# Local and global attention with a routed MLP: four transposes of the gate moved ahead of the output matmuls

## Chip, cores and metric

The kernel runs on one core of a Trainium2 chip. The metric is the device time of one execution in microseconds (us); the lower the better.

## What is computed

For 8 batches and 8 heads of width 64, 512 local tokens attend to a window of 32 tokens either side and to 32 global tokens; the 32 global tokens attend to everything. The 4352 resulting rows of 512 numbers then go through a gate (512 to 8), a greedy assignment of every row to one of 8 experts by sorted gate values, and the expert's two-layer MLP.

```
a_l = sm(where(|i-j| <= 32, scale * q_l @ k_l.T, -1e9) ++ scale * q_l @ k_g.T)
out_l = a_l @ concat(v_g, v_l)
out_g = sm(scale * q_g @ concat(k_g, k_l).T) @ concat(v_g, v_l)
x = concat(out_g, out_l) as rows of 512
logits = x @ w_gate ; greedy assignment, 544 rows for each of 8 experts
out[rows of e] = relu(x @ w1[e]) @ w2[e]
```

## The kernel before, in words

The program is written out in order for each engine, and each engine runs its own list in order. Attention comes first and takes the first 200 us of the trace; routing and the experts follow and are not touched.

Attention is a pipeline of 40 steps. Each batch has five: four local ones (a pair of heads each) and a global one. In iteration `i` three steps are worked on at once: the scores of step `i + 2` (`S`), the transposes of the probabilities of step `i` (`T0`, `T1`, one for each head, four 128x128 turns each), the masks and exponentials of step `i + 2` (`M0`, `M1`), and the output matmuls and normalisations of step `i - 1` (`O0`, `O1`). The order within an iteration is a string, `STEADY = "S T0 T1 M0 M1 O0 O1 G"`. TensorE (PE) does S, T, O; VectorE (DVE) the masks (L175), for a global step the maxima (L236 to L238), and the normalisations (L202 to L207, L278 to L282); ScalarE (ACT) the exponentials (L180, L244, L246) and the evacuation of the turns of p to `pt` and `pgt` (L314).

`G`, at the end of an iteration, does the pieces of the gate that are listed in `extra` for it. For each batch `b`, with `s0 = 5 * (b + 1)`:

- `gate_x` for c = 0 to 3, in iterations s0 to s0 + 3: four transposes of a column block of `xs` (the normalised outputs of a whole batch) into a PSUM tile `T`, and its evacuation to `xt` by DVE (L316, 682 ns);
- `turn_xg` in s0 + 1: one transpose of the global outputs `xg`, and its evacuation by DVE;
- `gate_m` in s0 + 4 (matmuls with the gate's weights, evacuated by ACT to `ltc`), and `gate_l` in s0 + 5 (four transposes of `ltc`, and a reduction on DVE to `L`). Iteration s0 + 5 is also the first of the next batch's `gate_x`;
- `gate_g` and its `gate_l` for the global rows once in four batches.

Batch 6 is compressed (two column blocks in each of iterations 35 and 36), and batch 7 has places of its own.

PSUM is full: three banks of `S`, three of `T`, two of `O`. A new `T` tile gets the bank that was released longest ago in program order; its first writer waits for the last reader of the tile that had the bank. Both heads of a step take a `T` tile each, a global step four, and `glob_scores` takes one too: the small scores `sb` of the second global head lie in a `T` tile from S on, until the last exponential of `M1` (L246) has read them. That is in iteration s0 + 2.

Loads and stores go out on SyncE's queue. Every PE instruction adds to a count of work (`tick`); each 0.62 us of it issues one piece of a load or store (`piece`), made to wait for the PE instruction before it (`paced`).

Of the kernel before, what the change touches and what calls it, by code (L numbers as in the profile page):

```python
# [13 lines left out]
ALU = mybir.AluOpType  # L14
AX = mybir.AxisListType
# [4 lines left out]
S = SL + SG  # L20
# [25 lines left out]
@with_exitstack  # L46
def block(ctx, tc, A, out, nbatch=B, dump=None):
    nc = tc.nc
    ctx.enter_context(tc.manual_schedule())
    consts = ctx.enter_context(tc.tile_pool(name="consts", bufs=1))  # L50
    dram = ctx.enter_context(tc.tile_pool(name="dram", bufs=1, space=DRAM))
    xd = dram.tile([N, DM], F32, name="xd")

    ident = consts.tile([128, 128], F32, name="ident")
    L = consts.tile([128, 34, E], F32, name="L")
    if dump is not None:
        nc.vector.memset(L, 0.0)
    rt = Routing(tc, A, consts, L, ident) if out is not None else None
    if rt:
        rt.begin(ctx)  # L60
    attention(tc, A, consts, xd, ident, L, nbatch, rt)
    if dump is not None:
        nc.sync.dma_start(dump["L"], L.rearrange("p a b -> p (a b)"))
        nc.sync.dma_start(dump["x"][:nbatch * S], xd[:nbatch * S])
    if out is not None:
        rt.begin_ps(ctx)
        experts(tc, A, xd, ident, rt, out)
# [3 lines left out]
def attention(ctx, tc, A, consts, xd, ident, L, nbatch, rt=None):  # L71
    nc = tc.nc
# [238 lines left out]
    def evac(dst, src, k):  # L311
        nev[k] += 1
        if who[k][nev[k] % len(who[k])] == "A" and not (k == "p" and nev[k] <= 2):
            nc.scalar.activation(dst, src, AF.Copy)  # L314
        else:
            nc.vector.tensor_copy(dst, src)  # L316

    def gate_x(src, xt, c, spare):
        t = ps.tile([128, NB, 128], F32, name="S" if spare else "T", bufs=3 if spare else 3)
        n = src.shape[1]  # L320
        for k in range(n):
            pe.transpose(t[:, k, :], src[:, k, c * 128:(c + 1) * 128], ident)
        evac(xt[:, c, :n * 128], t[:, :n].rearrange("p a b -> p (a b)"), "l" if late[0] else "x")

    def gate_m(xt, n):
        lt = ps.tile([128, 512], F32, name="T", bufs=3)
        for c in range(4):
            pe.matmul(lt[32 * c:32 * c + 32, :n * 128], wg[:, c, :], xt[:, c, :n * 128],
                             start=True, stop=True)
        ltc = wk.tile([128, 512], F32, name="ltc", bufs=2)  # L330
        evac(ltc[:, :n * 128], lt[:, :n * 128], "l")
        return ltc

    def gate_l(ltc, J, n):
        t = ps.tile([128, NB, 4, 32], F32, name="T", bufs=3)
        for k in range(n):
            pe.transpose(t[:, k].rearrange("p a b -> p (a b)"), ltc[:, k * 128:(k + 1) * 128], ident)
        nc.vector.tensor_reduce(L[:, J:J + n, :], t[:, :n, :, 0:8].rearrange("p k c e -> p k e c"),
                                axis=AX.X, op=ALU.add)

    def gate_d(xt, c):
        if c == 0:
            lt.append(ps.tile([128, NB, E], F32, name="T", bufs=3))
        for k in range(NB):
            pe.matmul(lt[0][:, k], xt[:, c, 128 * k:128 * k + 128], wg[:, c, 0:E], start=(c + k == 0), stop=(c + k == 6))
        if c == 3:
            nc.scalar.activation(L[:, 4 * nbatch - 4:4 * nbatch], lt[0], AF.Copy)
# [3 lines left out]
    def gate_units(b, src, J, n):  # L351
        xt = []

        def go(c):
            if c == 0:
                xt.append(wk.tile([128, 4, 128 * n], F32, name=f"xt{n}", bufs=1))
            if c < 4:
                gate_x(src(), xt[0], c, b == nbatch - 1)
            elif b == nbatch - 1:
                gate_d(xt[0], c - 4)  # L360
            elif c == 4:
                xt.append(gate_m(xt[0], n))
            else:
                gate_l(xt[1], J, n)
        return [lambda c=c: go(c) for c in range(8 if b == nbatch - 1 else 6)]

    late = [False]
    gxt = {}

    def turn_xg(b):  # L370
        if b % 4 == 0:
            gxt[b // 4] = wk.tile([128, 4, 128], F32, name="xt1", bufs=1)
        t = ps.tile([128, NB, 128], F32, name="S" if b == nbatch - 1 else "T", bufs=3)
        pe.transpose(t[:, 0, :], xg[b].rearrange("p a b -> p (a b)"), ident)
        q = 32 * (b % 4)
        evac(gxt[b // 4][:, :, q:q + 32], t[:, 0].rearrange("p (a b) -> p a b", a=4), "l" if late[0] else "x")

    def gate_g(i):
        gxt[i] = gate_m(gxt[i], 1)
# [8 lines left out]
    extra = {}  # L388

    def put(i, slot, f):  # L390
        extra.setdefault((i, slot), []).append(f)
    for b in range(nbatch):
        last = b == nbatch - 1
        s0 = 5 * (b + 1)
        put(s0 - 2 if last else s0 + 1, 0, lambda b=b: turn_xg(b))
        if b % 4 == 3:
            put(s0 - 1 if last else s0 + 3, 0, lambda b=b: gate_g(b // 4))
            put(s0 if last else s0 + 4, 0, lambda b=b: gate_l(gxt[b // 4], 32 + b // 4, 1))
        lo = gate_units(b, lambda b=b: xs[b], 4 * b, NB)
        if last:  # L400
            put(s0 - 3, 0, lo[0])
            put(s0 - 1, 0, lo[1])
            put(s0, 0, lo[2])
            for f in [lo[4], lo[3]] + lo[5:]:
                put(s0, 2, f)
        else:
            fast = b == nbatch - 2
            for k in range(4):
                put(s0 + (k // 2 if fast else k), 0, lo[k])
            put(s0 + (2 if fast else 4), 0, lo[4])  # L410
            put(s0 + (3 if fast else 5), 0, lo[5])

    LA = 2
    RAMP = 2
    START, STEADY = "T0 T1 O0 O1 S M0 M1 G", "S T0 T1 M0 M1 O0 O1 G"

    need, left = {}, {}
    for i, u in enumerate(steps):
        for q in [u[0].q] if isinstance(u[0], Local) else range(NP):
            for f, t in ((load_qk, i - LA), (load_v, i + 1)):  # L420
                k = f, u[0].b, q
# [8 lines left out]
    def used(f, u):  # L430
        for q in [u[0].q] if isinstance(u[0], Local) else range(NP):
            left[f, u[0].b, q] -= 1
            live[f] -= left[f, u[0].b, q] == 0

    now_ = [-LA]
# [32 lines left out]
    for i in range(-LA, ns + 1):  # L468
        if rt and i == 4:
            rt.load()  # L470
        if rt and i == 9:
            rt.prepare()
        nx = steps[i + LA] if i + LA < ns else []
        cur = steps[i] if 0 <= i < ns else []
        old = steps[i - 1] if i > 0 else []
        if i < RAMP:
            order = START
        else:
            order = STEADY
        late[0] = i >= ns - 1  # L480
        for n, what in enumerate(order.split()):
            now_[0] = i + n / 8
            if what == "S" and nx:
                (local_scores if isinstance(nx[0], Local) else glob_scores)(nx)
                used(load_qk, nx)
            if what[0] == "T" and cur:
                cur[int(what[1])].turn()
                cur[int(what[1])].take()
            if what[0] == "M" and nx:
                nx[int(what[1])].mask()  # L490
                nx[int(what[1])].exp()
            if what[0] == "O" and old:
                old[int(what[1])].out()
                if what[1] == "1":
                    used(load_v, old)
                old[int(what[1])].norm()
            if what == "G":
                if rt and i == ns:
                    for _ in first:
                        pass  # L500
                    rt.digits(slice(0, 28))
                for slot in range(3):
                    for f in extra.get((i, slot), []):
                        f()


WARM = 10
# [804 lines left out]
```

## Time and profile before

| | |
|---|---|
| median of 3 runs | 690.2 us (689.28 to 691.4) |
| the profiled execution | 689.55 us |
| its span, first to last instruction | 687.8 us |
| PE busy over the span | 642.6 us (93%) |
| DVE, ACT, GpSimd busy | 460.7 us (67%), 307.4 us (45%), 246.4 us (36%) |
| mean granted TensorE clock | 0.976 of full |

The engines are averaged over attention, routing and experts together; what a change in attention is worth has to be read from the first 200 us.

### The profile page before, as it was taken

The page shows a single profiled execution, that of the slowest core. Times are in us where ns is not written, and L with a number is a line of the kernel's source. Part 1 is how long each engine was busy: PE and PEld are TensorE (multiplying, and loading weights), DVE is VectorE, ACT ScalarE, POOL GpSimd, SP SyncE. Part 2 cuts the span into 40 slices and gives each one's busy share as a digit, 9 for nine tenths or more (in the row PEclk, how much of TensorE's full clock was granted, in tenths as well). Part 3 has the DMA queues.
Part 4 walks back from the last instruction along what each step waited for, and adds up shares of the span by engine and source line. Part 5 has one row for each costly group of instructions (what it writes and reads, how often), then busy time and mean ns, then how long its engine had stood idle before and what let it go on. Part 6 is the DMA issues. An engine that isn't in the chain of part 4 may idle for free.

```text
span 687.8 us, 24694 instructions
## 1 busy us (share of the span) xinstructions
PE 642.6 (93%) x10356; PEld 538.6 (78%) x10356; DVE 460.7 (67%) x1765; ACT 307.4 (45%) x828; POOL 246.4 (36%) x314
## 2 busy tenths in 40 slices
PE   7888999999982899999999999999999999999996
PEld 6676777767761798789789879878978978988985
DVE  4788788778876898777668758767857762640410
ACT  4776867777730352443333334334423343542410
POOL 4786667686600412411511330141141143312011
PEclk9999999999995799999999999999999999999999
DMA  7677878776210442603331440361352236431001
GB/s 242 206 244 226 227 228 242 242 218 200 89 68 2 137 175 91 255 32 124 110 144 39 143 177 22 128 202 48 124 163 91 80 114 238 134 127 54 9 15 51
DMA packets 41119, 93.91 MB, mean 137 GB/s; under 512 B 5424, under 2 KB 28208, under 8 KB 36912
## 3 DMA queue, kind: packets, MB, share of 16 engines
q0 software_dynamic: 10240, 51.39, 21.6%
q1 hardware_dynamic: 30768, 40.95, 19.5%
q8 instruction: 81, 1.33, 0.8%
q14 instruction: 30, 0.25, 0.1%
HBM read 74.49 MB, written 17.83 MB: 134 GB/s over the span
## 4 chain that ended last, share of the span: by engine, by line
PE 89%; DVE 4%; DMA 3%; issue 3%; ACT 1%; SPq 0%; POOLq 0%; POOL 0%; ACTq 0%
PE H L1135 29%; PE Y L1090 27%; PE T L90 11%; PE S L90 7%; PE O L90 7%; PE R L632 4%; PE H L967 2%; PE Y L1098 2%; DMA xg<-xd,idx 1%; DMA qk<-in_qk_dram 1%; DVE r_pm L554 1%; DMA mask<-in_mask_dram 1%; DVE r_G L554 0%; DMA out_dram<-y,idx 0%; DVE r_ce L554 0%
## 5 line engine op out<-in xcount | busy, mean ns | idle before, releaser
L1135 PE MATMUL H<-xh,w1h 128*128 128x272 f32 (+2 forms) x512 | 149.8, 294 | 0.9 <-DVE hl L554 0.6
L1135 PE MATMUL H<-xh,w1l 128*128 128x272 f32 (+2 forms) x512 | 149.9, 294 | 0.0
L1135 PE MATMUL H<-xl,w1h 128*128 128x272 f32 (+2 forms) x512 | 148.4, 291 | 0.0
L979 POOL DMA_INDIRECT out_dram<-y,idx x40 | 40.8, 1019 | 179.4 <-ACT y L1078 102.8
L1137 ACT ACTIVATE hh<-H 128x272 fp32r<-128x272 f32 (+2 forms) x128 | 50.8, 397 | 119.4 <-PE H L1135 115.9
L1090 PE MATMUL Y<-w2h,hh 128*128 128x512 f32 x256 | 103.7, 405 | 0.0
L1090 PE MATMUL Y<-w2l,hh 128*128 128x512 f32 x256 | 103.5, 404 | 0.0
L1090 PE MATMUL Y<-w2h,hl 128*128 128x512 f32 x256 | 103.4, 404 | 0.0
L1135 PEld LDWEIGHTS H<-xh,w1h 128*128 128x128 f32 x512 | 96.3, 189 | 2.3 <-DVE hl L554 1.4
L1135 PEld LDWEIGHTS H<-xl,w1h 128*128 128x128 f32 x512 | 96.3, 188 | 0.5
L1135 PEld LDWEIGHTS H<-xh,w1l 128*128 128x128 f32 x512 | 96.1, 188 | 0.5
L126 POOL COPY vw<-vw 32x650 f32<-32x650 f32 x96 | 69.3, 722 | 52.4 <-DMA vw<-in_vw_dram 33.7
L180 ACT ACTIVATE p<-p,nm 128x128 f32<-128x128 f32 x256 | 78.0, 397 | 8.5 <-DVE nm L175 8.5
L1078 ACT ACTIVATE y<-Y 128x512 f32<-128x512 f32 (+1 forms) x40 | 21.3, 533 | 122.9 <-PE Y L1090 79.5
L554 DVE SCALAR_TENSOR_TENSOR hl<-H,hh 128x272 fp32r<-128x272 f32 (+2 forms) x128 | 55.1, 434 | 30.6 <-ACT h L1139 18.6
L175 DVE CUSTOM_DVE_ANT_0 p<-S,mask 128x128 f32<-128x128 f32 x256 | 56.5, 286 | 24.2 <-PE S L90 22.8
L90 PE MATMUL S<-qk 64*32 64x128 f32 (+2 forms) x2240 | 52.6, 293 | 9.3 <-issue 5.1
L554 DVE TENSOR_TENSOR w2l<-w2r,w2h 128x512 fp32r<-128x512 f32 x64 | 42.8, 682 | 25.3 <-ACT w2h L933 25.3
L920 POOL DMA_INDIRECT xg<-xd,idx x40 | 42.9, 1073 | 37.4 <-DVE idx L554 23.2
L1090 PEld LDWEIGHTS Y<-w2h,hh 128*128 128x128 f32 x256 | 48.1, 188 | 10.4 <-issue 1.2
L1090 PEld LDWEIGHTS Y<-w2h,hl 128*128 128x128 f32 x256 | 48.2, 188 | 9.3
L1090 PEld LDWEIGHTS Y<-w2l,hh 128*128 128x128 f32 x256 | 48.2, 188 | 9.0
(180 smaller groups left out, 1116.4 us busy)
## 6 DMA issues: line engine op xcount, KB each, us to landing
qk<-in_qk_dram SPq DMA_DIRECT2D x64, 204.0 KB, 3.0
vw<-in_vw_dram SPq DMA_DIRECT2D x64, 162.5 KB, 3.3
xd<-xs SPq DMA_DIRECT2D x28, 256.0 KB, 3.4
qk<-in_qk_dram SPq DMA_DIRECT2D x32, 200.0 KB, 3.2
xd<-xs SPq DMA_DIRECT2D x1, 1024.0 KB
xg<-xd,idx POOLq DMA_INDIRECT x40
out_dram<-y,idx POOLq DMA_INDIRECT x40
vw<-in_ve_dram SPq DMA_DIRECT2D x32, 16.2 KB, 3.8
```

The costliest lines, as they stand in the source:

```text
L90: s.last = op(o, w, x, **kw)
L126: copy(bv[32 * g:32 * g + 32], av[32 * g + 32:32 * g + 64])
L175: nc.vector.tensor_tensor_reduce(s.p[:, c, :], s.st[:, c, :], mask[:, c, :], -SCALE, BIG, ALU.add, ALU.min, s.nm[:, c:c + 1])
L180: nc.scalar.activation(s.p[:, c, :], s.p[:, c, :], AF.Exp, bias=s.nm[:, c:c + 1], scale=-1.0)
L554: return op(*args, **kw)
L632: s.nc.tensor.matmul(out, *args, **kw)
L920: nc.gpsimd.indirect_dma_start(out=dst, out_offset=None, in_=src, element_offset=off, in_offset=bass.IndirectOffsetOnAxis(ap=idx, axis=0))
L979: nc.gpsimd.indirect_dma_start(out=out4 if t == 4 else out, out_offset=bass.IndirectOffsetOnAxis(ap=rt.idx[ph][:, k:k + 1], axis=0), in_=y ...
L1078: nc.scalar.activation(y, p[:, :w], AF.Copy)
L1090: nc.tensor.matmul(p, h[:, f, q], w[f], start=(f + k == 0), stop=(f + k == 9))
L1135: nc.tensor.matmul(p, w[d][:, fs], x[:, d, q], start=(n == 0), stop=(n == 11))
L1137: nc.scalar.activation(hh[:, f, q], p, AF.Relu)
```

## The change

The four transposes of `gate_x` get a place of their own in the order, `X`, straight behind `T1`; their evacuation gets another, `Y`, behind `O1`. This holds for c = 0 to 3 of batches 0 to 5 and c = 0 and 2 of batch 6, 26 in all. Everything else of the gate stays in `G`, and so do the transposes of batch 7 and c = 1 and 3 of batch 6. `gate_x` and `gate_l` now return their evacuation, which `G` calls at once. The fraction of an iteration that the load planner uses as its clock is in tenths now, in the steady order, and not in eighths.

```diff
@@ gate_x
-        evac(xt[:, c, :n * 128], t[:, :n].rearrange("p a b -> p (a b)"), "l" if late[0] else "x")
+        k = "l" if late[0] else "x"
+        return lambda: evac(xt[:, c, :n * 128], t[:, :n].rearrange("p a b -> p (a b)"), k)
@@ gate_l
-        nc.vector.tensor_reduce(L[:, J:J + n, :], t[:, :n, :, 0:8].rearrange("p k c e -> p k e c"),
-                                axis=AX.X, op=ALU.add)
+        return lambda: nc.vector.tensor_reduce(L[:, J:J + n, :], t[:, :n, :, 0:8].rearrange("p k c e -> p k e c"),
+                                               axis=AX.X, op=ALU.add)
@@ gate_units, go
-                gate_x(src(), xt[0], c, b == nbatch - 1)
+                return gate_x(src(), xt[0], c, b == nbatch - 1)
...
-                gate_l(xt[1], J, n)
+                return gate_l(xt[1], J, n)
@@ attention
-                put(s0 + (k // 2 if fast else k), 0, lo[k])
+                put(s0 + (k // 2 if fast else k), 0 if fast and k % 2 else "X", lo[k])
...
-    START, STEADY = "T0 T1 O0 O1 S M0 M1 G", "S T0 T1 M0 M1 O0 O1 G"
+    START, STEADY = "T0 T1 O0 O1 S M0 M1 G", "S T0 T1 X M0 M1 O0 O1 Y G"
...
-            now_[0] = i + n / 8
+            now_[0] = i + n / len(order.split())
+            if what == "X":
+                turned = [f() for f in extra.get((i, "X"), [])]
+            if what == "Y":
+                for f in turned:
+                    f()
...
-                        f()
+                        f = f()
+                        if f:
+                            f()
```

## Rows read from the trace of the kernel before

**Rows 1.** The page: the chain that ended last, share of the span by line.

```profile
PE H L1135 29%; PE Y L1090 27%; PE T L90 11%; PE S L90 7%; PE O L90 7%; PE R L632 4%; PE H L967 2%; PE Y L1098 2%; DMA xg<-xd,idx 1%; DMA qk<-in_qk_dram 1%; DVE r_pm L554 1%; DMA mask<-in_mask_dram 1%; DVE r_G L554 0%; DMA out_dram<-y,idx 0%; DVE r_ce L554 0%
```

**Rows 2.** Four steps of attention: busy us (instructions) of each engine, clock, DMA.

```profile
88.50:105.62 17.12, 16.76 (x539) 12.61 (x537) 14.60 (x82) 13.82 (x43) 10.64 (x17) 1.00 0.70 216
```

**Rows 3.** Waits of PE and its weight loads, 20 to 200 us: us, times, longest.

```profile
PE S L90 <- issue: 5.1, 7, 1.3
...
PEld S L90 <- DMA qk<-in_qk_dram: 1.7, 2, 0.8
...
PEld T L90 <- DVE xt L316: 0.2, 1, 0.2
```

**Rows 4.** Weight loads in order of time, iterations 16 to 19: start, us, [idle before].

```profile
88.50 0.86 PEld L90 LDWEIGHTS T<-ident,p 128*128 128x128 f32 x8 [0.20 <-issue]
...
91.26 0.27 PEld L90 LDWEIGHTS S<-qk 64*32 64x32 f32 x24 [0.17 <-issue]
...
92.39 0.85 PEld L90 LDWEIGHTS T<-ident,p 128*128 128x128 f32 x8
93.41 0.95 PEld L90 LDWEIGHTS O<-vw,pt 128*32 128x32 f32 x64 [0.17 <-issue]
94.46 0.42 PEld L90 LDWEIGHTS T<-ident,xs 128*128 128x128 f32 x4
95.04 0.82 PEld L90 LDWEIGHTS S<-qk 64*32 64x32 f32 x51 [0.17 <-ACT pg L244]
96.10 0.18 PEld L90 LDWEIGHTS S<-qk 64*32 64x32 f32 x13 [0.24 <-issue]
96.48 0.85 PEld L90 LDWEIGHTS T<-ident,p 128*128 128x128 f32 x8 [0.20 <-issue]
...
100.89 1.08 PEld L90 LDWEIGHTS T<-ident,pg 128*128 128x128 f32 x10 [0.20 <-ACT p L180]
102.24 0.20 PEld L90 LDWEIGHTS T<-ident,pg 128*128 128x128 f32 x2 [0.27 <-ACT pgt L314]
102.61 0.95 PEld L90 LDWEIGHTS O<-vw,pt 128*32 128x32 f32 x64 [0.17 <-issue]
...
104.51 0.91 PEld L90 LDWEIGHTS S<-qk 64*32 64x32 f32 x64 [0.84 <-issue]
105.62 0.85 PEld L90 LDWEIGHTS T<-ident,p 128*128 128x128 f32 x8 [0.20 <-ACT p L180]
```

**Rows 5.** The same in an early iteration that has nothing in G.

```profile
26.27 0.95 PEld L90 LDWEIGHTS O<-vw,pt 128*32 128x32 f32 x64 [0.17 <-issue]
27.32 0.14 PEld L90 LDWEIGHTS S<-qk 64*32 64x32 f32 x3
```

**Rows 6.** DVE in order of time, iterations 16 to 19.

```profile
88.60 0.29 DVE L175 CUSTOM_DVE_ANT_0 p<-S,mask 128x128 f32<-128x128 f32 x1 [1.85 <-PE S L90]
...
90.30 0.16 DVE L202 TENSOR_SCALAR ls<-O 128x4 f32<-128x4 f32 x1
...
91.78 0.88 DVE L316 COPY xt<-T 128x128 f32<-128x128 f32 x2
92.58 0.65 DVE L236 TENSOR_REDUCE gm<-S 128x1 f32<-128x480 f32 x1
...
94.46 0.15 DVE L202 TENSOR_SCALAR ls<-O 128x4 f32<-128x4 f32 x1
...
95.94 0.68 DVE L316 COPY xt<-T 128x512 f32<-128x512 f32 x1
96.72 0.29 DVE L175 CUSTOM_DVE_ANT_0 p<-S,mask 128x128 f32<-128x128 f32 x1
...
103.34 0.16 DVE L202 TENSOR_SCALAR ls<-O 128x4 f32<-128x4 f32 x1 [0.43 <-PE O L90]
```

**Rows 7.** ACT in order of time, iteration 17.

```profile
93.08 1.09 ACT L314 ACTIVATE pt<-T 128x512 f32<-128x512 f32 x2 [0.42 <-PE T L90]
...
95.63 0.33 ACT L246 ACTIVATE pg<-T,gm 128x64 f32<-128x64 f32 x1
```

## The prediction

> **What bounds the kernel now.** I read the chain that ended last first: within attention it is PE alone that appears with weight, T 11%, S 7% and O 7% of the span [rows 1]. Then four iterations in the middle of attention, 88.50 to 105.62: PE is busy 16.76 of 17.12 us, DVE 14.60, ACT 13.82 [rows 2]. So PE sets the pace, and DVE follows closely. What PE waits for is hardly ever another engine: scores wait 5.1 us in all for nothing that the profile shows ("issue"), 1.7 us for a load, and turns 0.2 us for an evacuation by DVE [rows 3]. The weight loads in order of time give the pitch of every part of an iteration [rows 4], and DVE's and ACT's lists beside them show how late the readers of the T tiles run [rows 6, 7].
>
> **What the change takes away.** 26 groups of four turns move; each instruction stays. Eight turns and the step to the outputs last 93.41 - 92.39 = 1.02 us, with 0.17 idle before the outputs: (1.02 - 0.17) / 8 = 0.107 for a turn [rows 4]. Four turns of xs behind the outputs last 95.04 - 94.46 = 0.58, which is 4 x 0.107 = 0.43 and 0.15 for the step from whole-array turns back to tiled scores. The outputs last 1.05 before turns (94.46 - 93.41) and 1.05 before scores (27.32 - 26.27) [rows 4, 5], so once the turns follow those of p, that 0.15 is gone: T T X O S has one step fewer than T T O X S. It goes only where G holds no other PE work. In s0 + 1 the turn of xg stays there, in s0 (from batch 1 on) the turns of ltc, in iteration 23 gate_g, and in 35 and 36 several. Left are iteration 5, six at s0 + 2 and five at s0 + 3: 12 x 0.15 = 1.8 us.
>
> The rows show these steps as idle weight loads of 0.17 to 0.20 [rows 4]. [...]
>
> **What it adds: the outputs come 0.43 us later.** They are behind the moved turns now, so O0's result comes at 1.45 + 0.73 = 2.18 us after the first turn of p (1.02 + 0.43; 0.73 is 103.34 - 102.61, outputs to DVE's first read) [rows 4, 6]. DVE's list is unchanged: masks 1.70 (88.60 to 90.30) or global maxima 1.88 (92.58 to 94.46), two normalisations 1.48 (94.46 to 95.94), the evacuation 0.78 to the next instruction (95.94 to 96.72) and 0.68 by itself [rows 6]. In iteration 16 the masks end at 1.80 after T0; DVE will stand idle to 2.18. That delay of 0.38 goes into the evacuation of xt, and two things now wait for readers of T tiles. Take iterations 16 to 19, and T0 of 16 as zero.
>
> Iteration 16 (s0 + 1). Normalisations 2.18 to 3.66, evacuation of xs to 4.34, of xg behind it. PE: outputs from 1.45 to 2.50, the turn of xg and the step to S 0.107 + 0.17, global scores 92.39 - 91.26 = 1.13 [rows 4]: T0 of 17 could start at 3.91 (before: 3.89). But sb takes the bank of T1, xg that of T0, so T0 of 17 gets the bank of the moved turns, whose reader ends at 4.34. With 0.05 allowed for the signal (my estimate; without it every wait below is 0.05 shorter) it starts at 4.39, 0.50 later than before. Before, T0's bank was xg's, read earlier than xs.
>
> Iteration 17 (s0 + 2). One bank holds sb until L246 has read it, 95.63 + 0.33 - 92.39 = 3.57 after T0 [rows 4, 7]. The moved turns come when only T0's bank is free, and its evacuation starts 0.69 after T0 (93.08 - 92.39) [rows 4, 7]. The row nearest to this wait is that of the global step, where a turn waits for the evacuation of a tile filled just before: the turn starts 102.24 - 100.89 = 1.35 after the first [rows 4]. The moved turns would follow at 0.86, so PE stands 0.48. Queued behind them: both outputs, so both normalisations. Before, the same turns, on the same bank, came at 94.46, behind the outputs, and waited for nothing. Iteration: 1.34 + 0.43 + 0.17 + 1.05 + 1.11 = 4.10 (S 1.11: 105.62 - 104.51) [rows 4]. Before it lasted 4.09 with an idle 0.24 in S; if that stays too, the price is 0.25.
>
> Iteration 18 (s0 + 3). 1.45 + 1.05 + 1.11 = 3.61, against 1.02 + 1.05 + 0.58 + 1.11 = 3.76. DVE runs late meanwhile: in 17 its normalisations begin at 1.94 + 0.73 = 2.67, the next masks at 2.67 + 1.48 + 0.78 = 4.93, which is 0.83 into 18; they end at 2.53, and the evacuation at 2.53 + 1.48 + 0.68 = 4.69, 1.08 into 19.
>
> Iteration 19 (global, s0 + 4). Its third T tile has the bank of 18's moved turns: 1.13 instead of 6 x 0.107 = 0.64. Of this 0.49, the 0.27 that the fourth tile waited anyway is covered; 0.22 remains. Then DVE has no xt to evacuate, and its delay is gone.
>
> Sum for the batch: 0.50 + 0.25 - 0.15 + 0.22 = 0.82 us slower. **Bounds.** Below: iterations 16 to 20 took 17.12 us [rows 2], with 0.24 and, in iteration 18, 4.41 - 3.76 = 0.65 of idle time that no engine caused. If such gaps fall while DVE catches up, waits of up to that size cost nothing, and only the saved steps remain, 0.30 a batch at s0 + 2 and s0 + 3: from -0.30. Above: 0.82 with all gaps besides. I take 0.60, nearer the upper end, since half of the gaps or more would fall elsewhere. Six batches (0 to 5) have the pattern: 6 x 0.60 = 3.6, less 0.15 for iteration 5. **+3.5 us.**
>
> **What moves at no cost.** The moved turns issue no DMA themselves, but their ticks do: a piece of a load may go out half an iteration earlier, and the planner's clock runs in tenths. SyncE's queue stays in order, each piece still behind a PE instruction. The loads' slack covers it: scores waited twice for qk, 1.7 us in all [rows 3]; without that cover a late load cost 0.8. The reduction of gate_l and all ACT work keep their places. PE's clock was granted in full throughout these steps [rows 2], and gaps of half a microsecond do not lengthen the longest that it had (1.3) [rows 3].
>
> Against the profiled execution of 689.55 us the sum gives 693.05. That execution is 0.65 below the median of the three; I put the forecast between, at **693.3 us**.
>
> **Rivals.**
> 1. *The issue gaps take the waits' place.* For it: 5.1 us of them before scores alone [rows 3], and 0.89 in the four iterations above, about the size of 0.82. Against it: they would have to fall behind the outputs of s0 + 1 or within s0 + 2. Time: the four iterations go from 17.12 to 17.12 - 0.89 + 0.82 = 17.05 plus the gaps that stay outside, so from -1.8 us to +2 in all, about 690.
> 2. *Fewer steps between tilings decide; faster.* If the turn of xg or ltc left in G costs PE less than a whole step, all 26 groups save 0.15: 3.9 us, 686.3; with the 12 alone 688.4. It decides from the point where the two waits of s0 + 1 and s0 + 2 fall under (3.9 - 2.1) / 6 = 0.3 us a batch together, of the 0.98 reckoned above. For it: turns waited for xt once, 0.2 us [rows 3]. Against: DVE's starts follow each other without a gap from 88.60 to 96.72 [rows 6], and the 0.48 for ACT does not hang on DVE.
> 3. *The moved turns of s0 + 2 get sb's bank.* They would start at 3.57 + 0.05 instead of 0.86 (8 x 0.107), 2.76 us for PE, six times: 16.6 us, 707. Against: before, the turns at 94.46 ran while L246 still had to read sb at 95.63 [rows 4, 7], so they had another bank.
>
> [...]
>
> **How the numbers follow.** Chances: the waits bind (forecast, 691.5 to 695.5) 0.47; rival 1 0.33; rival 2 0.16; rival 3 0.04. Faster or slower by over 0.3% (2.07 us, about what this kernel's measurement can tell from no change) means under 688.1 or over 692.3: faster 0.16, same 0.33, slower 0.51. The range leaves out rival 3, most of rival 2 and a little above: 688.0 to 695.8; the likeliest case's own is 691.5 to 695.5.
>
> **What would show it.** Right: in s0 + 1 to s0 + 2 the weight loads of T0 wait some 0.5 us for DVE's xt; in s0 + 2 the turns of xs wait about 0.5 for ACT's pt; at s0 + 3 outputs go to scores in 1.05 with nothing between; DVE waits for O about 0.4 in s0 + 1. Wrong: the wait for xt stays at some tenths of a microsecond in all; or attention ends earlier though the waits are there, which would mean that the gaps shrank. A different bank for the turns, or loads that come late by the planner's new clock, would make the sum wrong outright.

## The result and the profile after

The change takes 695.29 us (median of 17 runs) where the kernel before takes 691.4 beside it (17 runs): ratio 1.0067, 95% interval 1.005 to 1.0084, slower. At 690 us that is 4.6 us, with 3.5 to 5.8 by the interval; the two medians alone, from which the ratio is not formed, lie 3.9 apart. The forecast was 3.5 against the profiled execution, at the lower end of the interval. Of the 2.0 us between the forecast of 693.3 and 695.29, 1.2 lie in the kernel before, whose median was 690.2 when the forecast was made. The profiled execution of the change is a long one among its runs (699.22 us, span 697.4), so single times of its trace are compared by their places, and sizes by several profiles.

The weight loads in order of time, iterations 16 to 19 of the change; they answer to [rows 4].

```profile
94.86 0.86 PEld L90 LDWEIGHTS T<-ident,p 128*128 128x128 f32 x8 [0.20 <-issue]
95.69 0.47 PEld L90 LDWEIGHTS T<-ident,xs 128*128 128x128 f32 x4
96.33 0.95 PEld L90 LDWEIGHTS O<-vw,pt 128*32 128x32 f32 x64 [0.17 <-issue]
...
99.34 0.85 PEld L90 LDWEIGHTS T<-ident,p 128*128 128x128 f32 x8 [0.70 <-PE T L90]
100.69 0.42 PEld L90 LDWEIGHTS T<-ident,xs 128*128 128x128 f32 x4 [0.49 <-ACT pt L314]
101.27 0.95 PEld L90 LDWEIGHTS O<-vw,pt 128*32 128x32 f32 x64 [0.17 <-issue]
102.32 0.89 PEld L90 LDWEIGHTS S<-qk 64*32 64x32 f32 x64
103.40 0.85 PEld L90 LDWEIGHTS T<-ident,p 128*128 128x128 f32 x8 [0.20 <-issue]
...
105.92 0.57 PEld L90 LDWEIGHTS S<-qk 64*32 64x32 f32 x35
107.94 0.39 PEld L90 LDWEIGHTS S<-qk 64*32 64x32 f32 x29 [1.45 <-issue]
108.54 1.07 PEld L90 LDWEIGHTS T<-ident,pg 128*128 128x128 f32 x10 [0.20 <-issue]
109.88 0.20 PEld L90 LDWEIGHTS T<-ident,pg 128*128 128x128 f32 x2 [0.27 <-ACT pgt L314]
...
113.26 0.86 PEld L90 LDWEIGHTS T<-ident,p 128*128 128x128 f32 x8 [0.20 <-ACT p L180]
```

Both waits stand where the prediction put them. T0 of s0 + 2 (99.34) waits 0.70, where no idle time stood before (92.39 in [rows 4]); then the turns of xs wait 0.49 for `pt`. The idle time of 0.70 carries the name "PE T", but those turns had long ended; VectorE's list shows what did end then:

```profile
97.06 0.16 DVE L202 TENSOR_SCALAR ls<-O 128x4 f32<-128x4 f32 x1 [0.31 <-PE O L90]
...
98.55 0.88 DVE L316 COPY xt<-T 128x512 f32<-128x512 f32 x2
...
102.00 0.16 DVE L202 TENSOR_SCALAR ls<-O 128x4 f32<-128x4 f32 x1 [0.69 <-PE O L90]
```

The copy of xs begins at 98.55 and takes 0.68 by itself [rows 6], to 99.23; T0 starts at 99.34. VectorE, which had no idle time at these places before, stands for the outputs 0.31 and 0.69.

The four iterations, from one first turn to the next, in us. "Less gaps" leaves out issue idle time before scores and outputs beyond the usual 0.2 (before 0.24 and 0.65, after 1.51: scores took 108.54 - 105.92 = 2.62 instead of 1.11).

| | before, less gaps | forecast, undiscounted | after, less gaps |
|---|---|---|---|
| s0 + 1 | 3.89 | 4.39 | 4.48 |
| s0 + 2 | 3.85 | 4.10 | 4.06 |
| s0 + 3 | 3.76 | 3.61 | 3.63 |
| s0 + 4 | 4.73 | 4.95 | 4.72 |
| sum | 16.23 | 17.05 | 16.89 |

With the gaps the same stretch took 17.12 us before [rows 2], and now:

```profile
94.86:113.26 18.40, 16.37 (x539) 12.50 (x537) 14.70 (x82) 13.82 (x43) 11.63 (x18) 1.00 0.66 200
```

The same instructions on PE and VectorE, the clock granted in full, and 1.28 us more. Nearly all of the difference between the two profiled executions lies ahead of routing, whose first matmul starts at 210.9 us (before 202.3): 8.6 of the 9.6 us between the spans. From there to the end they take 486.5 and 485.5 us. These two executions lie further apart than the kernels do.

### The profile page after: what moved, and what is told of

It reads as the page before. It is cut to its first block, busy times and chain, and to the rows that moved or that the text cites. A ratio compares the mean times of both kernels' runs of the same rounds, so it can differ in the third digit from the quotient of the medians.

```text
span 697.4 us, 24703 instructions
## 1 busy us (share of the span) xinstructions
PE 644.3 (92%) x10356; PEld 540.1 (77%) x10356; DVE 461.4 (66%) x1765; ACT 308.2 (44%) x828; POOL 246.9 (35%) x314
## 4 chain that ended last, share of the span: by engine, by line
PE 85%; DVE 6%; issue 3%; DMA 2%; POOL 1%; ACT 1%; SPq 1%; POOLq 0%; ACTq 0%; DVEq 0%
PE H L1143 28%; PE Y L1098 27%; PE T L90 9%; PE O L90 6%; PE S L90 5%; PE R L640 4%; PE H L975 2%; PE Y L1106 2%; DMA vw<-in_vw_dram 1%; PE Y L1176 1%; DVE r_pm L562 1%; POOL vw L126 1%; DVE xs L207 1%; DVE r_G L562 1%; ACT pt L314 1%
## 5 line engine op out<-in xcount | busy, mean ns | idle before, releaser
L1098 PEld LDWEIGHTS Y<-w2h,hh 128*128 128x128 f32 x256 | 48.2, 188 | 10.6 <-issue 1.2
```

The costliest lines, as they stand in the source:

```text
L1098: nc.tensor.matmul(p, h[:, f, q], w[f], start=(f + k == 0), stop=(f + k == 9))
```

## The experiments

Three theories went into the expectations. Theory 1: the two waits for the readers of `T` tiles make the difference. Theory 2: the loads, which the planner's new clock issues at other times, make it. Theory 3: TensorE's issue gaps make it. These turned out to recur at every 256th instruction of its list (a weight load and its matmul are two); the rows are in the last section.

### Each wait taken away, and both

`evac_early`: the evacuation ahead of O0, so that VectorE reads the tile before it waits for outputs.

```diff
-    START, STEADY = "T0 T1 O0 O1 S M0 M1 G", "S T0 T1 X M0 M1 O0 O1 Y G"
+    START, STEADY = "T0 T1 O0 O1 S M0 M1 G", "S T0 T1 X M0 M1 Y O0 O1 G"
```

> The evacuation of the moved turns stands in front of the outputs' normalisations on VectorE (Y ahead of O0) instead of behind them; PE and ACT keep the order of the changed kernel. Theory 1, waits for T tiles: VectorE fills the 0.4 us in which it stood idle for the outputs, the bank is free 1.2 us earlier, so the turns of p in iteration s0 + 2 wait for nothing (0.5 us a batch back) and the third tile of the global step neither (0.2); the wait of the turns of xs for pt stays (0.49). Six times 0.7 us off 695.3: about 691 us, ratio to before 0.999 to 1.003. Theory 2, the loads: the pieces go out at other places and PE's issue gaps grow; VectorE's order does not touch that, ratio stays at 1.005 to 1.008.

`s0_2_undone`: the turns of c = 2 alone go back into G.

```diff
-                put(s0 + (k // 2 if fast else k), 0 if fast and k % 2 else "X", lo[k])
+                put(s0 + (k // 2 if fast else k), 0 if (k % 2 if fast else k == 2) else "X", lo[k])
```

> Only the moved turns of iteration s0 + 2 (c = 2 of batches 0 to 5) go back to the end of the iteration; the other 20 stay in front of the outputs. Theory 1: the wait of these turns for pt is gone (0.49 less the 0.15 of the saved step), and VectorE is 0.6 us earlier in the step after, so the global step's third tile does not wait (0.2); the wait of p's turns for xt at the start of s0 + 2 stays (0.5). Per batch 0.3 to 0.4 us above before instead of 0.8: ratio 1.002 to 1.004. If only the wait for xt counts, 1.006; if only the wait for pt counts, 1.000. Theory 2, the loads: little changes, 1.005 to 1.008.

`both_undone`: both edits.

> Evacuation in front of O0, and the turns of c = 2 back at the end of their iteration: neither of the two waits is left, and six of the twelve saved steps (0.15 us each) go too. Theory 1: the time of the kernel before or slightly under it, ratio 0.998 to 1.002, iterations 10 to 34 less gaps about 110. Theory 3: the gaps stay larger than the 7.1 us of before (9 or more in those iterations), ratio 1.002 to 1.005 although no wait is left.

| | ratio to before | 95% | median, us | before beside it, us |
|---|---|---|---|---|
| the change | 1.0067 | 1.005 to 1.0084 | 695.29 | 691.4 |
| evac_early | 1.0046 | 1.0018 to 1.0074 | 696.99 | 693.24 |
| s0_2_undone | 1.0034 | 1.0002 to 1.0067 | 696.62 | 693.24 |
| both_undone | 0.9993 | 0.9971 to 1.0016 | 691.93 | 691.71 |

A median is to be read only against the kernel before beside it. `evac_early` missed its range (0.999 to 1.003): taking the larger wait away gave back less than expected. `s0_2_undone` and `both_undone` lie in theirs.

The waits of the weight loads of turns from 20 to 205 us (us, times, longest), for the change, for `evac_early` and for `s0_2_undone`:

```profile
PEld T L90 <- PE T L90: 3.6, 7, 0.7
PEld T L90 <- ACT pt L314: 2.9, 6, 0.5
```

```profile
PEld T L90 <- ACT pt L314: 2.9, 6, 0.5
```

```profile
PEld T L90 <- PE T L90: 3.6, 6, 0.7
```

Each edit removes its own wait whole and leaves the other; `both_undone` has neither row. Its weight loads in s0 + 2 and the next first turn:

```profile
94.83 0.85 PEld L90 LDWEIGHTS T<-ident,p 128*128 128x128 f32 x8
95.86 0.95 PEld L90 LDWEIGHTS O<-vw,pt 128*32 128x32 f32 x64 [0.17 <-issue]
96.90 0.42 PEld L90 LDWEIGHTS T<-ident,xs 128*128 128x128 f32 x4
97.49 0.99 PEld L90 LDWEIGHTS S<-qk 64*32 64x32 f32 x64 [0.17 <-ACT pg L244]
98.68 0.85 PEld L90 LDWEIGHTS T<-ident,p 128*128 128x128 f32 x8 [0.20 <-issue]
```

With both waits gone the whole 0.74% is gone, though three quarters of the turns are still in their new place: theory 1. This was run at one place of the instruction list only. The single shares are less sure: the early evacuation gives 0.21 or 0.41%, the return of c = 2 gives 0.33 or 0.53%, each with an interval of some 0.3 either way.

### The loads

`loads_as_before`: PE, VectorE and ScalarE keep the order of the change, while loads are issued in the order, and by the clock, of the kernel before.

```diff
+    STEP = "S T0 T1 M0 M1 O0 O1 G".split()
...
-            now_[0] = i + n / len(order.split())
+            now_[0] = i + CLOCK.get(what, n / 8)
...
+                work0, pe.tick = pe.work, None
...
+                for _ in range(n0):
+                    pe.work += 2 * 128 / 2400
+                    tick()
```

> PE, VectorE and ScalarE in the order of the changed kernel, but every load and store goes out in the order of the kernel before: the work of the moved turns is counted for the load planner where they stood before, and its clock runs in eighths with the old places. Theory 1, waits for T tiles: nothing is gained, ratio 1.005 to 1.008. Theory 2, the loads: the issue gaps of PE go back, ratio 0.999 to 1.002.

Ratio 1.0065 (1.004 to 1.009): as slow as the change. Theory 2 falls, and the prediction's zero for the loads stands.

### A version that should have kept the saved steps

`paired_early`: early evacuation, c = 0 and 1 turned together in s0, c = 2 and 3 in s0 + 3, the turn of xg ahead of the outputs.

```diff
-        put(s0 - 2 if last else s0 + 1, 0, lambda b=b: turn_xg(b))
+        put(s0 - 2 if last else s0 + 1, "X" if b < nbatch - 2 else 0, lambda b=b: turn_xg(b))
...
-                put(s0 + (k // 2 if fast else k), 0 if fast and k % 2 else "X", lo[k])
+                put(s0 + (k // 2 if fast else (0, 0, 3, 3)[k]), 0 if fast and k % 2 else "X", lo[k])
```

> Moved turns only where no T bank is short: c = 0 and 1 both in s0, c = 2 and 3 both in s0 + 3, the turn of xg in s0 + 1 in front of the outputs too, all evacuations ahead of the normalisations. s0 + 2 has no gate work left. Theory 1: none of the waits of the changed kernel, and the step from whole-array turns to tiled scores falls away in s0 + 1, s0 + 2 and s0 + 3: 3 x 0.15 x 6 = 2.7 us under before, ratio 0.995 to 0.998. If the saved steps are worth nothing, 1.000. Theory 2, the loads: the turns still move ahead with their pieces, 1.004 to 1.008.

Ratio 1.004 (1.0011 to 1.0069): a miss. Its weight loads in s0 + 2 show a part of what took the gain:

```profile
96.51 0.13 PEld L90 LDWEIGHTS S<-qk 64*32 64x32 f32 x2 [0.51 <-ACT pg L244]
```

Without the turns in between the scores reach their bank before ScalarE's exponential has read it. The turns of xs were PE's filler for that time; before, the wait there was 0.17 [rows 4]. From 20 to 205 us these waits sum to 3.1 us, six times (before 1.3, six times): 1.8 us more. That takes most of the 2.7 us hoped for, but leaves open why the version is 0.4% slower than the kernel before.

### Where every 256th instruction falls

Small matmuls behind the warm-up push the rest of TensorE's list on by 64, 128 or 192 instructions (16, 32, 48 matmuls, in the traces 32, 64, 96 weight loads with as many passes), so that the issue gaps fall elsewhere in the period.

```diff
     for _ in range(WARM):
         pe.matmul(wt[:, 0, :], warm, warm, start=True, stop=True)
+    for _ in range(32):
+        pe.matmul(wt[0:32, 1, 0:8], warm[:, 0:32], warm[:, 0:8], start=True, stop=True)
```

> The kernel before, with 16 tiny matmuls (32 columns of weights, 8 columns) behind the warm-up, which move every later PE instruction 64 places down its list. Theory 1 (waits for T tiles make the whole difference): as before, ratio 0.998 to 1.002. Theory 3 (PE's issue gaps stand at every 256th instruction of its list, where new instructions come in; in the profiles taken so far they add up to 11.3 us before and 14.4 to 15.6 in the four variants, which makes 3 to 4 us): the gaps move by 32 weight loads, to other operations; if their sum hangs on where they fall, it leaves 11.3 by 2 us or more and the ratio goes with it, 0.99 to 1.01; if it hangs on the order of the work, it stays at 11 to 12.

> The same with 32 tiny matmuls, 128 places, half of the distance of the gaps. Theory 1: ratio 0.998 to 1.002. Theory 3: the gaps move by 64 weight loads; sum of the gaps 2 us or more off 11.3 if the place decides, 11 to 12 if the order of the work decides.

> 48 small matmuls behind the warm-up, that is 96 weight loads and 96 matmuls in TensorE's list: its issue gaps fall 192 instructions later (64 and 128 are known). Theory 1 (waits for T tiles make the difference): within 0.3% of the kernel before, as no wait changes; attention's iterations 10 to 34 less their gaps stay at 110.2 to 110.9 us. Theory 3 (issue gaps): the gaps in those iterations sum to another value than 7.1, between 7 and 10, and the ratio goes with it, 1.000 to 1.006.

> The changed kernel with the same 16 tiny matmuls behind the warm-up. Theory 1: ratio to before 1.005 to 1.008, as unpadded. Theory 3: if the place of the gaps decides, their sum leaves 15.5 and the ratio lies anywhere from 1.000 to 1.010; if the order of the work decides (outputs and scores back to back use instructions faster), the sum stays at 15 and the ratio at 1.005 to 1.008.

> The changed kernel with 32 tiny matmuls, 128 places. Theory 1: 1.005 to 1.008. Theory 3: as in the run with 64 places; the difference of the two padded pairs, after less before at the same padding, is what the order costs with the place taken out: 0 to 2 us if the place decides, 3 to 5 us if the waits and the order decide.

> The changed order with its issue gaps 192 instructions later. Theory 1: the distance to before_pad192 is 5 us (iterations 10 to 34 less gaps 112.7 against 110.4, and the batch ahead of them), ratio about 1.007. Theory 3: the distance is that of the gaps as well, anything between 0.3% and 1%; the mean distance over the four places 0, 64, 128 and 192 is the price of the order, about 6 us by the three known.

> The order with the evacuation in front of the normalisations, and 64 places of padding as before: at the same place of the gaps as before_pad64 (ratio 1.0016) and after_pad64 (1.0104). Theory 1: the late evacuation is what the change costs, so it lies within 1.5 us of before_pad64, ratio 1.000 to 1.004, with no wait for xt in the profile and 0.49 for pt in each s0 + 2. Theory 3, by which outputs and scores back to back let the gaps grow: it lies with after_pad64 or half way, 1.005 to 1.010, with a gap sum as in after_pad64, 3 us above before_pad64.

> The same with 128 places, beside before_pad128 (1.0063) and after_pad128 (1.015). Theory 1: 1.004 to 1.008. Theory 3: 1.010 to 1.015.

> The changed order with the evacuation in front of O0, issue gaps 192 instructions later. Theory 1: the larger of the two waits is gone, iterations 10 to 34 less gaps 110 to 112 us, distance to before_pad192 at most 2 us (0.3%). Theory 3: distance between 0 and 0.5%, as at the other three places; mean over the four about 0.3%.

Ratios to the kernel before without padding:

| moved by | before | the change | evac_early | change - before |
|---|---|---|---|---|
| 0 | 1 | 1.0067 | 1.0046 | 0.67% |
| 64 | 1.0016 (0.999 to 1.0041) | 1.0104 (1.0071 to 1.0137) | 1.0061 (1.0034 to 1.0088) | 0.88% |
| 128 | 1.0063 (1.0038 to 1.0088) | 1.015 (1.0122 to 1.0177) | 1.0063 (1.0041 to 1.0086) | 0.87% |
| 192 | 1.0053 (1.0029 to 1.0077) | 1.0116 (1.0082 to 1.015) | 1.0112 (1.0078 to 1.0146) | 0.63% |
| mean | 1.0033 | 1.0109 | 1.0071 | 0.76% |

Padding alone costs up to 0.6% before and 0.8% after, so theory 1's "no change" for the padded kernel before was missed at 128 and at 192, and so was its 1.005 to 1.008 for the change at 64 and 128. It is no clean test of place: the granted clock differs too (0.72 from 20 to 30 us in `before_pad64`, where it is 1.00 before). It is not clear that padding causes this, since a second profile of the kernel before has 0.83 there. The difference between the orders hardly depends on the padding: 0.63 to 0.88%, mean 0.76%, 5.3 us (6.0 by the medians), each padded one uncertain by some 0.4%.

`evac_early` keeps 0.38% of it, on average half, but unevenly: 0.46, 0.45, 0 and 0.59%. At 64 (1.000 to 1.004 expected) and at 192 (at most 0.3% expected) it missed what theory 1 said. Without the issue gaps its iterations 10 to 34 last 111.1 us on average (110.0, 111.9, 112.2, 110.5), between 110.4 in the order of before and 113.5 in that of the change (table below). So by the rows 2.4 of 3.1 us come back, by the time only half of the difference; why they differ is open.

### Less store traffic

During attention the stores of xs are cut to 64 of 512 columns in batches 0 to 6, to see whether the traffic makes the gaps. The other columns are filled in after attention with those of batch 7, so the experts work on wrong rows; the kernel is of use for times only.

```diff
-            paced(xd[r:r + 128, :], xs[b][:, k])
+            paced(xd[r:r + 128, 0:64], xs[b][:, k, 0:64])
```

> The kernel before with stores of xs cut to 64 of 512 columns in batches 0 to 6 (the other columns of x are filled from batch 7's rows once attention is over, so the experts read wrong rows): 6.4 MB less traffic during attention, as many instructions. If the issue gaps are instructions that come late because loads and stores keep the transfer engines busy, their sum from iteration 10 to 34 falls from 7.1 us to under 5; if not, it stays. The total time says little, since the filling comes behind attention.

> The changed kernel with the same cut. The time less that of before_short_store is what the change costs with small gaps. Theory 1: 4 us or more, and iterations 10 to 34 without their gaps last 2 to 3 us longer than in before_short_store. Theory 3: the gaps' part goes, so 2 to 3 us remain.

Ratios 0.9951 (0.9925 to 0.9977) and 1.0064 (1.0037 to 1.0092). DMA falls from 216 to 180 GB/s from 60 to 180 us (in the windows of `before_short_store`):

```profile
60.00:180.00 120.00, 111.61 (x3646) 85.93 (x3633) 95.35 (x542) 89.95 (x272) 88.79 (x134) 1.00 0.63 180
```

The gaps of iterations 10 to 34 are 8.1 and 8.8 us all the same (before 7.1, the change 8.1), where under 5 was expected if the traffic made them. A sixth less traffic does not shrink them; more than that isn't shown. The orders lie 1.1% apart here by the ratios, 5.7 us (0.8%) by the medians. Why the order of before gains 0.5% from the cut and that of the change nothing is open.

### The same two programs, profiled once more

> The kernel before, unchanged, profiled a second time. Theory 3 (the place of every 256th instruction sets the issue gaps): they fall at the same instructions as in the first profile, and their sum in iterations 10 to 34 is again 7.1 us within 1. If the sum of one profile is chance, the same places with another sum, 8 to 11 us. Iteration time less gaps 110 to 111 us either way (theory 1).

> The change, unchanged, profiled a second time. Theory 1: the waits of s0 + 1 and s0 + 2 are the same to 0.1 us, iteration time less gaps 112 to 113 us. Theory 3: gaps sum again to 8.1 us within 1. If the sum of one profile is chance: another sum, 9 to 13 us, with the same places.

Iterations 10 to 34 in us, worked out from the weight loads. A gap is idle time over 0.28 that the profile puts down to issue, less 0.18 of it; ahead of the scores behind the gate's matmuls, where 0.84 is usual, only what exceeds that counts.

| | duration | gaps | rest |
|---|---|---|---|
| before, first and again | 118.0, 121.6 | 7.1, 9.8 | 110.9, 111.9 |
| the change, first and again | 120.8, 124.3 | 8.1, 10.6 | 112.7, 113.7 |
| mean of 6 profiles in the order of before | 120.0 | 9.6 (7.1 to 13.1) | 110.4 |
| mean of 7 in the order of the change | 124.3 | 10.9 (8.1 to 13.0) | 113.5 |
| both_undone | 123.4 | 11.4 | 112.0 |

(Six: before twice, its three paddings, the short store. Seven: the same of the change, and `loads_as_before`.) The gaps fall at the same instructions in both profiles of one program, though not each is over 0.28 in both, and their sum differs by 2.7 and 2.5 us. So the gap sum of one profile does not belong to a program, and theory 3, as an account of this change, isn't shown: `both_undone` had more gaps than the mean of the change (11.4) and still the time of the kernel before. Three more idle times of `both_undone` (0.65, 0.74 and 1.06) stand at places of the same series of 256, where the profile names another engine; with them its gaps are 13.3 and its rest 110.1, that of the order of before. The means give 4.3 us for five batches, 0.86 a batch, about 3 of it outside the gaps.

## Why the direction was right and the size too small

The terms are compared over iterations 10 to 34, less gaps, in the ten profiles that had the clock granted in full there: five in the order of before (the first, paddings of 64, 128 and 192, the short store) and five in that of the change (both profiles, the padding of 64, the short store, `loads_as_before`).

| | forecast | batch shown | mean of ten profiles |
|---|---|---|---|
| s0 | 0 | | -0.03 |
| s0 + 1 | 0.50 | 0.59 | 0.49 |
| s0 + 2 | 0.25 | 0.21 | 0.23 |
| s0 + 3 | -0.15 | -0.13 | -0.19 |
| s0 + 4 | 0.22 | -0.01 | 0.08 |
| sum | 0.82 | 0.66 | 0.58 |

- **The waits** were right in mechanism and size. Both come in all five batches of the change: T0 waits 0.62 on average, the turns of xs 0.49. No run shows the 0.05 allowed for the signal: T0 starts 0.11 behind the end of the copy (99.23 to 99.34).
- **The saved step** came too. In the change the outputs go to scores in 102.32 - 101.27 = 1.05 with nothing between. The idle 0.17 ahead of the scores in [rows 4] went with the step.
- **s0 + 4** was too large. The forecast had VectorE's evacuation end 1.08 after T0 of this iteration. In the first profile of the change it ends 0.35 to 0.71 after it in four of the five batches, and what the turns wait for it is covered by their next wait, for ScalarE's evacuation: behind that the turns start 1.34 after T0 in every batch, as they did before. The batch behind the one shown is an example (131.05 + 0.68 and 132.41, against 131.07):

```profile
131.05 0.68 DVE L316 COPY xt<-T 128x512 f32<-128x512 f32 x1
131.07 1.14 PEld L90 LDWEIGHTS T<-ident,pg 128*128 128x128 f32 x10 [0.20 <-ACT p L180]
132.41 0.20 PEld L90 LDWEIGHTS T<-ident,pg 128*128 128x128 f32 x2 [0.20 <-ACT pgt L314]
```

In the batch shown the evacuation ends 0.60 ahead of T0, since a gap of 1.45 in s0 + 3 let VectorE catch up. This is the one place where rival 1's mechanism shows.

- **The step that failed** is "I take 0.60, nearer the upper end": it takes 0.22 off the sum, because issue gaps would fall away while VectorE catches up. They didn't shrink. By the means above they come to 9.6 us in the order of before and 10.9 in that of the change: 0.25 a batch more and not 0.22 less, though they scatter by more than this from profile to profile. The series stands at every 256th instruction whatever the waits, and in the batch shown the gap behind the two waits was 1.45 (107.94) where 0.60 stood before (100.31 in the line below). With its gaps a batch is 0.72 (ten profiles) to 0.86 us (all thirteen) longer. That would make 4.2 to 5.0 us for six batches, less 0.15 for iteration 5 as in the forecast; measured are 4.6 as it stands and 5.3 over four places of the list.

```profile
100.31 0.39 PEld L90 LDWEIGHTS S<-qk 64*32 64x32 f32 x27 [0.60 <-issue]
```

- **Luck.** Without the gaps a batch is 0.58 longer, which is close to the 0.60 taken. It is no success of the discount: the term of s0 + 4 was too large by about as much as the discount took away.
- **Rival 2** (faster) fails at its own condition: the two waits would have had to be under 0.3 a batch, and T0's delay of 0.59 and the 0.49 before the turns add to 1.08. **Rival 3** falls with the same 0.49, which would have been 2.76.
- **VectorE's pace.** VectorE does not set the pace of whole steps: it stands idle for outputs more than before. It holds TensorE up at one place of a batch, where T0 of s0 + 2 waits for its copy (0.70 in the batch shown). The idle time from 20 to 205 us of the change (before: 7.2 us, 17 times):

```profile
DVE ls L202 <- PE O L90: 16.2, 26, 2.5
```

- **Open.** Of 0.86 a batch by the means of all thirteen profiles, 0.61 lies outside the gaps, lower granted clock included, and 0.25 in gaps whose scatter between profiles is larger. Whether a wait makes a later gap longer, or chance did, isn't settled. No version beat the kernel before.

## What to carry to other kernels

Before a producer is moved ahead of something, list which buffer it takes, who reads that buffer last, and where this reader stands in its own engine's order: here the turns moved and their reader did not, and that cost more (waits of 0.62 and 0.49 us a batch) than the steps between turns and scores saved (0.15 each, two a batch). Work that "could go earlier" may be filler for a wait of another engine; `paired_early` took it away and met the wait. When half a per cent matters, shift the instruction list of both versions and profile each twice: some small matmuls ahead of the list moved the time by up to 0.8%, and the gaps of one program differed by 2.7 us between two profiles.

## What the runs showed of the hardware

**Issue gaps at every 256th instruction.** The weight loads of the kernel before from one gap to the next (first group), and the second profile of the same program at the same scores (second group):

```profile
83.69 1.15 PEld L90 LDWEIGHTS O<-vw,pgt 128*32 128x32 f32 x75 [0.58 <-issue]
84.93 0.42 PEld L90 LDWEIGHTS T<-ident,ltc 128*128 128x128 f32 x4
85.31 0.47 PEld L90 LDWEIGHTS T<-ident,xs 128*128 128x128 f32 x4
85.95 0.64 PEld L90 LDWEIGHTS S<-qk 64*32 64x32 f32 x44 [0.17 <-issue]
87.94 0.36 PEld L90 LDWEIGHTS S<-qk 64*32 64x32 f32 x20 [1.35 <-issue]
```

```profile
91.26 0.36 PEld L90 LDWEIGHTS S<-qk 64*32 64x32 f32 x20 [2.18 <-issue]
91.82 1.13 PEld L90 LDWEIGHTS T<-ident,p 128*128 128x128 f32 x8 [0.20 <-issue]
93.28 1.72 PEld L90 LDWEIGHTS O<-vw,pt 128*32 128x32 f32 x64 [0.33 <-issue]
```

75 + 4 + 4 + 44 = 127 weight loads with as many matmuls lie between two gaps, about 256 instructions; the gap before the last 20 weight loads of the scores is 1.35 us in one profile and 2.18 in the other. The page of the change lists a queue for instructions (packets, MB, share):

```profile
q8 instruction: 81, 1.33, 0.8%
```

These are 81 packets of 16.4 KB, and TensorE's 2 x 10356 = 20712 weight loads and matmuls, divided by 256, are 80.9. The packets keep TensorE's pace too: in the kernel before, 43 come from 20 to 200 us, beside 5382 matmuls and 5380 weight loads (250 instructions to a packet), and 16 from 202.3 to 400 us, beside 2 x 2088 (261). That this queue brings TensorE's instructions alone is not shown. Not every place of the series has a gap: in iterations 10 to 34 of before there are 15 over 0.28 us, 7.1 in all, where a batch has five such places.

**The clock after a gap.** The second profile of before from 91.50 on, behind that gap of 2.18 us:

```profile
91.50:97.20 5.70, 5.70 (x129) 4.31 (x113) 4.10 (x24) 3.53 (x10) 5.21 (x9) 0.70 0.57 191
```

The granted clock is 0.70 on average, after 1.00 from 84.70 to 91.20: eight turns take 1.13 us instead of 0.86, the outputs 1.72 instead of 0.95. Behind a gap of 2.77 us in the change it stayed at 1.00 (94.86:113.26 above), so the gap alone does not decide:

```profile
94.31 0.36 PEld L90 LDWEIGHTS S<-qk 64*32 64x32 f32 x21 [2.77 <-issue]
```
